# The second MLP product of the last two token groups from seven quarter products in place of eight

## The chip, the cores and the metric

The kernel runs on one core of a Trainium2 chip. The metric is the device time of one execution in microseconds (us). Three timed runs of the kernel before gave 926.75, 925.68 and 925.69 us, median 925.69 us.

## The reference

A causal attention with a window of 128 positions and a linear distance bias, followed by an MLP with SiLU, all in float32:

```
scores = scale * q @ k.T;  scores = where(0 <= rel < 128, scores + bias, -1e9)
attn = exp(scores - max);  attn = attn / (sum(attn) + 1e-9)
x = (attn @ v).transpose(0, 2, 1, 3).reshape(4608, 512)
h = x @ w_in                      # 4608 x 2048
g = h * (1 / (1 + exp(-h)))
out = g @ w_out                   # 4608 x 512
```

There are 8 batches of 8 heads, 576 positions and head size 64. Only the last line of the MLP, `g @ w_out`, is computed in another way by the change.

## The kernel before

The 4608 tokens are cut into 9 groups of 512 (`TG`), counted here from 0 to 8. A group has 16 steps (`NF`), one for each 128 of the 2048 hidden columns; the text writes step 7.3 for step 3 of group 7, and the code numbers steps through, `n = 16 * g + f`. A step has these parts:

- `gemm1`, 12 products on PE (TensorE), in two halves: 128 hidden columns of 512 tokens into a PSUM tile `h`. From group 2 on every operand is split into two fp16 parts, a high and a low one, and a product is made of three: high by high, high by low, low by high.
- `act1` on ACT (ScalarE): the tanh of `h` into the SBUF tile `gt`. `act2` on DVE (VectorE): `(gt + 1) * h`. `act3` on ACT: the fp16 part `gh`. `act4` on DVE: the fp16 rest `gl`.
- `gemm2`, 12 products: for each of four blocks of 128 tokens `gh` by the high part of `w_out`, `gh` by its low part, `gl` by the high part, each 512 columns wide, summed over the 16 steps in one PSUM bank for each block (tags w, x, y, z, one buffer each). After the last step `store` scales the four tiles and sends them out.

Each product is a weight load (LDWEIGHTS, 128 columns) and a MATMUL. In the order that is written out by hand, `gemm2` of step n-1 follows `gemm1` of step n, so that the activation of step n has the time of a `gemm2` and the next `gemm1` to finish. At the end of a group both remaining `gemm2` follow the last `gemm1`; at its start two `gemm1` stand together.

The order is a list of positions, four to a step, at each of which PE gets half of a `gemm1` or a `gemm2`. A table (`plan`, filled by `put` and `ahead`) says what else is issued at a position. The attention for group g+1 is laid between the steps of group g, one pair of heads-and-tokens (`p`) every 8 positions, that is every two steps: scores on PE, masked row maximum on DVE (L469), exponentials on ACT (L479), splits on ACT (L488) and DVE (L493), a transpose by DMA, the product with v on PE (L543), normalising on DVE (L561 to L570) and two fp16 parts (L580, L142). Queries and keys of the later batches are split on ACT (L385) and DVE (L391), v on POOL (GpSimd, L415) and DVE (L421). Group 8 has no attention beside it. All engines work through their queues in order.

The lines to follow are gemm1 L650 (L655 in the first two groups), act1 L666, act2 L671, act3 L681, act4 L687, gemm2 L719, and the stores L730 to L739.

Of the kernel before, what the change touches and what calls it, by code (L numbers as in the profile page):

```python
# [91 lines left out]
def tile_window_attention_then_silu_mlp(ctx, tc, qk, qk16, v, w_in, w_out, distance, out):  # L92
# [534 lines left out]

    hps, gact, ops = {}, {}, {}

    def gemm1(n, half):  # L630
# [4 lines left out]
        if n // NF >= IN16:
            g, w = n // NF, w16[0, f]
            for cc in (2 * half, 2 * half + 1):
                seq += [(0, 0, cc), (0, 1, cc), (1, 0, cc)]
            for i, (wp, xp, cc) in enumerate(seq):
                start, stop = half == 0 and i == 0, half == 1 and i == len(seq) - 1  # L640
                c = xp * NCC + cc
                if g > IN16:
# [6 lines left out]
                for k, (o, x) in enumerate(moves):
                    nc.tensor.matmul(o, w[:, wp, cc], x, start=start and k == 0, stop=stop, skip_group_check=True)  # L650
# [12 lines left out]
    def act1(n):  # L663
        gt = pool.tile([P, TG], F32, tag="gt", name=f"gt{n}")
        scale = 0.5 / W_SCALE if n // NF < IN16 else gsc[n // NF][:, 0:1]
        nc.scalar.activation(gt, hps[n], AF.Tanh, scale=scale)  # L666
        gact[n] = gt

    def act2(n):
        gt = gact[n]  # L670
        nc.vector.scalar_tensor_tensor(out=gt, in0=gt, scalar=1.0, in1=hps[n], op0=ALU.add, op1=ALU.mult)  # L671

    def act3(n):
        gt = gact[n]
        dt = F32R if n // NF < OUT16 else F16
        gh = pool.tile([P, TG], dt, tag="gh", name=f"gh{n}")
        gl = pool.tile([P, TG], dt, tag="gl", name=f"gl{n}")
        if n // NF < OUT16:
            (nc.vector.tensor_copy if at_edge(n) else nc.scalar.copy)(gh, gt)  # L679
        else:  # L680
            nc.scalar.activation(gh, gt, AF.Copy, scale=CUT)  # L681
        gact[n] = (gh, gl, gt)

    def act4(n):
        gh, gl, gt = gact[n]
        if n // NF >= OUT16:
            nc.vector.scalar_tensor_tensor(out=gl, in0=gt, scalar=CUT, in1=gh, op0=ALU.mult, op1=ALU.subtract)  # L687
            return
        minus(nc.vector if at_edge(n) or n < NF else nc.gpsimd, gl, gt, f32(gh))

    def turn_over(n):
# [8 lines left out]
        if more:  # L700
            x_parts(i, 1)
            for k in range(1, GT):
                x_parts(i + k, 0)
                x_parts(i + k, 1)

    def gemm2(n, half):
        g, f = divmod(n, NF)
        for ti in (2 * half, 2 * half + 1):
            if f == 0:
                ops[ti] = psum.tile([P, DM], F32, tag="wxyz"[ti], name=f"o{g}_{ti}")  # L710
            gh, gl, _ = gact[n]
            t = slice(ti * P, (ti + 1) * P)
            if g < OUT16:
                hi, lo = weight("woh", f), weight("wol", f)
            else:
                hi, lo = w16[1, f][:, 0], w16[1, f][:, 1]
            seq = [(gh, hi), (gh, lo), (gl, hi)]
            for i, (a, w) in enumerate(seq):
                nc.tensor.matmul(  # L719
                    ops[ti], a[:, t], w, start=(f == 0 and i == 0), stop=(f == NF - 1 and i == len(seq) - 1),  # L720
                    skip_group_check=True,
                )
# [344 lines left out]
```

## Time and profile before

| | |
|---|---|
| median of three runs | 925.69 us |
| the profiled execution's own time | 926.23 us |
| its span from the first to the last instruction | 924.4 us |
| PE busy | 914.6 us (99%) |
| DVE busy | 645.0 us (70%) |
| ACT busy | 559.6 us (61%) |
| POOL busy | 116.0 us (13%) |
| TensorE clock granted | 1.00 of full speed |

How it is read: a busy share is an average over stages. A product is shown with the time from its start to the end of its results (0.38 us for 512 columns), while the next one starts before that; what a product costs is therefore read from the distance of two starts. "Idle before" is the time an engine stood still ahead of an instruction, and behind the arrow stands what ended it. In the views in order of time, equal instructions that follow each other are merged into one row with their count.

### The profile page before, as it was taken

The numbers are of one execution on the slowest core, as the hardware profiler recorded it, in microseconds if no ns is written. First come the engines' busy times: TensorE is split into PE (matmuls) and PEld (weight loads), VectorE is DVE, ScalarE is ACT, GpSimd is POOL, SyncE is SP. The second block draws the span as 40 slices with busy tenths as digits, with TensorE's granted clock in tenths as the row PEclk, the third lists the DMA queues.
The fourth block names the chain that finished last, engine by engine and source line by source line (L and its number), as shares of the span: only waits on it lengthen the run. The fifth ranks groups of instructions, "written<-read, shape, count | busy, mean of one in ns | idle before, by whom it ended". The sixth has DMA issues, their size and how long they took to land.

```text
span 924.4 us, 17093 instructions
## 1 busy us (share of the span) xinstructions
PE 914.6 (99%) x6426; PEld 572.4 (62%) x6426; DVE 645.0 (70%) x1629; ACT 559.6 (61%) x1149; POOL 116.0 (13%) x115
## 2 busy tenths in 40 slices
PE   9999999999999999999999999999999999999998
PEld 8867777777787886555555555555555555544443
DVE  6889876446776778888788778666867777743222
ACT  7778997675556764666677755555655565533222
POOL 2343442222221220000000000000000000000000
PEclk9999999999999999999999999999999999999999
DMA  8977825243275645434598736444545454211001
GB/s 311 392 189 225 256 57 129 69 91 80 71 218 152 178 115 137 114 94 112 114 247 219 203 88 163 112 103 104 160 115 115 114 160 113 65 35 52 1 1 45
DMA packets 197747, 122.89 MB, mean 133 GB/s; under 512 B 166432, under 2 KB 166816, under 8 KB 197664
## 3 DMA queue, kind: packets, MB, share of 16 engines
q1 hardware_dynamic: 197376, 121.54, 49.3%
q8 instruction: 50, 0.82, 0.4%
q14 instruction: 33, 0.27, 0.1%
q10 hardware_dynamic: 288, 0.26, 0.1%
HBM read 71.96 MB, written 9.44 MB: 88 GB/s over the span
## 4 chain that ended last, share of the span: by engine, by line
PE 85%; DVE 5%; ACT 1%; issue 1%; ACTq 0%
PE o L719 38%; PE h L650 29%; PE h L655 8%; PE av L543 4%; PE sp L439 3%; PE sp L446 2%; DVE gt L671 1%; DVE hr L493 1%; DVE t L469 0%; DVE w L816 0%; DVE vmx L204 0%; ACT t L479 0%; DVE x L142 0%; ACT w L804 0%; DVE wr L810 0%
## 5 line engine op out<-in xcount | busy, mean ns | idle before, releaser
L719 PE MATMUL o<-w,gh 128*128 128x512 f16 (+1 forms) x1152 | 351.2, 386 | 0.0
L650 PE MATMUL h<-xt,w 128*128 128x512 f16 (+1 forms) x1536 | 310.5, 353 | 0.0
L650 PEld LDWEIGHTS <-w 128*128 128x128 f16 x1536 | 144.6, 98 | 125.8 <-issue 2.2
L666 ACT ACTIVATE gt<-h,gsc 128x512 f32<-128x512 f32 x112 | 77.0, 687 | 239.8 <-PE h L650 237.7
L719 PE MATMUL o<-w,gl 128*128 128x512 f16 (+1 forms) x576 | 221.6, 385 | 0.2 <-DVE gl L142 0.2
L671 DVE SCALAR_TENSOR_TENSOR gt<-gt,h 128x512 f32<-128x512 f32 x144 | 98.7, 686 | 147.3 <-ACT gt L666 146.8
L719 PEld LDWEIGHTS <-gh 128*128 128x128 f16 x768 | 74.8, 98 | 89.1
L479 ACT ACTIVATE t<-t,mx 128x256 f32<-128x256 f32 (+1 forms) x288 | 125.2, 486 | 5.2 <-DVE mx L469 5.0
L493 DVE SCALAR_TENSOR_TENSOR hr<-t,hr 128x512 f16<-128x512 f32 (+1 forms) x128 | 89.3, 703 | 29.7 <-ACT hr L488 29.6
L687 DVE SCALAR_TENSOR_TENSOR gl<-gt,gh 128x512 f16<-128x512 f32 x96 | 66.8, 696 | 42.4 <-ACT gh L681 41.3
L655 PE MATMUL h<-xh,w 128*128 128x512 f32 x256 | 89.8, 405 | 0.0
L719 PEld LDWEIGHTS o<-w,gh 128*128 128x128 f32 x384 | 69.8, 188 | 15.3 <-DVE vsc L264 0.3
L415 POOL TENSOR_SCALAR v<-rv,vsc 128x512 f16<-128x512 f32 x30 | 25.2, 841 | 427.8 <-DMA rv<-v 351.8
L681 ACT ACTIVATE gh<-gt 128x512 f16<-128x512 f32 x96 | 60.4, 629 | 28.1 <-DVE gt L671 23.7
L488 ACT ACTIVATE hr<-t 128x512 f16<-128x512 f32 (+1 forms) x128 | 71.4, 595 | 1.4 <-DVE hr L493 1.4
L719 PEld LDWEIGHTS <-gl 128*128 128x128 f16 x384 | 37.6, 98 | 46.2 <-DVE gl L687 1.2
L543 PEld LDWEIGHTS <-hl 128*128 128x128 f16 x1464 | 51.4, 98 | 16.5 <-issue 5.2
L469 DVE CUSTOM_DVE_ANT_0 t<-sp,tab,vsc 128x256 f32<-128x256 f32 (+1 forms) x144 | 58.5, 461 | 1.8 <-PE sp L439 1.4
L140 POOL TENSOR_TENSOR gl<-gt,gh 128x512 fp32r<-128x512 f32 x30 | 38.6, 1286 | 164.2 <-ACT gh L679 148.9
L543 PE MATMUL av<-v,hl 128*128 128x65 f16 (+1 forms) x1464 | 54.8, 193 | 1.6 <-DVE mx L469 1.5
L655 PEld LDWEIGHTS h<-xh,w 128*128 128x128 f32 x256 | 48.1, 188 | 12.3 <-issue 0.2
L469 DVE CUSTOM_DVE_ANT_0 t<-sp,tab 128x256 f32<-128x256 f32 (+1 forms) x144 | 50.1, 402 | 3.3 <-PE sp L446 2.9
(135 smaller groups left out, 1006.5 us busy)
## 6 DMA issues: line engine op xcount, KB each, us to landing
r<-qk SPq DMA_DIRECT2D x36, 512.0 KB, 3.9
qs<-qk SPq DMA_DIRECT2D x18, 512.0 KB, 5.1
out<-ot SPq DMA_DIRECT2D x35, 256.0 KB, 2.4
wr<-w_in SPq DMA_DIRECT2D x16, 512.0 KB, 6.7
wr<-w_out SPq DMA_DIRECT2D x16, 512.0 KB, 6.2
rv<-v SPq DMA_DIRECT2D x30, 256.0 KB, 4.0
vm<-v SPq DMA_DIRECT2D x27, 256.0 KB, 5.0
q<-qk SPq DMA_DIRECT2D x18, 256.0 KB, 3.3
```

The costliest lines, as they stand in the source:

```text
L469: nc.vector.tensor_tensor_reduce(out=st[p]["t"][u][:, h, 2 * P - n :], in0=st[p]["sp"][h][:, u, o].rearrange("p o c -> p (o c)"), in1=tab[ ...
L479: nc.scalar.activation(x, x, AF.Exp, bias=st[p]["mx"][:, 2 * u + h : 2 * u + h + 1], scale=-1.0)
L488: nc.scalar.activation(split_of(p, u, hr)[:, 0], t[:, :, 2 * P - n :], AF.Copy, scale=PSCALE)
L493: nc.vector.scalar_tensor_tensor(out=hr[:, 1], in0=t[:, :, 2 * P - n :], scalar=PSCALE, in1=hr[:, 0], op0=ALU.mult, op1=ALU.subtract)
L543: nc.tensor.matmul(av[:, 2 * u + h, : rhs.shape[-1]], lhs, rhs, start=(n == 0), stop=(n == len(seq) - 1), skip_group_check=True,)
L650: nc.tensor.matmul(o, w[:, wp, cc], x, start=start and k == 0, stop=stop, skip_group_check=True)
L655: nc.tensor.matmul(hps[n], w[:, cc], x, start=(half == 0 and i == 0), stop=(half == 1 and i == len(seq) - 1), skip_group_check=True,)
L666: nc.scalar.activation(gt, hps[n], AF.Tanh, scale=scale)
L671: nc.vector.scalar_tensor_tensor(out=gt, in0=gt, scalar=1.0, in1=hps[n], op0=ALU.add, op1=ALU.mult)
L681: nc.scalar.activation(gh, gt, AF.Copy, scale=CUT)
L687: nc.vector.scalar_tensor_tensor(out=gl, in0=gt, scalar=CUT, in1=gh, op0=ALU.mult, op1=ALU.subtract)
L719: nc.tensor.matmul(ops[ti], a[:, t], w, start=(f == 0 and i == 0), stop=(f == NF - 1 and i == len(seq) - 1), skip_group_check=True,)
```

## The change

In groups 7 and 8 (`FAST`) `gemm2` uses a scheme of seven products for a 2 by 2 split of both operands. The tokens are taken 256 at a time (two blocks of 128), the hidden columns as pairs of blocks j and j+8, the output columns in two halves of 256. A step now is one pair j for one 256 tokens: 8 steps for the first 256 tokens, then 8 for the second. `gemm1_fast` fills the same PSUM tile `h` with block j+8 in the first half and block j in the second, in 24 products of 256 columns. `act2` adds three instructions on DVE, which form five sums and differences of the four blocks; `act3` and `act4` work on seven blocks in two instructions each (256 and 640 columns). `gemm2_fast` makes 7 times 3 products of 256 columns into four PSUM banks (the seven sums, two to a bank). After 8 steps `store_fast` joins the seven sums to four quarters: two copies on ACT and eight instructions on DVE, half of them behind the first four products and the rest behind the others, and sends two tiles of 128 by 512.

The sums of w_out's quarters that the seven products need are made at eight places in groups 4 (its last position) to 6 (`SUMS`, `SUMS_STEP`): each has seven instructions on POOL, two on ACT and two on DVE, and puts its fp16 results into buffers that are free by then.

In the order, step 8 of such a group keeps `gemm2` of step 7 behind it, step 9 has no `gemm2`, and step 10 has those of steps 8 and 9; the rest is as before.

```diff
+FAST = (NG - 2, NG - 1)
+SUMS, SUMS_STEP = 316, 16
...
+    def sum_float(j):
+        wsum["r"] = r = pool.tile([P, 2, DM], F32, tag="big", name=f"wr{j}")
+        for k in range(2):
+            w = w16[1, j + k * HALF_F]
+            nc.gpsimd.tensor_add(r[:, k], w[:, 0], w[:, 1])
+
+    def sum_make(j):
...
+        nc.gpsimd.tensor_sub(q[:, 0], b12, b22)
+        nc.gpsimd.tensor_sub(q[:, 1], b21, b11)
+        nc.gpsimd.tensor_add(q[:, 2], b11, b22)
+        nc.gpsimd.tensor_add(q[:, 3], b21, b22)
+        nc.gpsimd.tensor_add(b11, b11, b12)
...
+    def sum_hi(j):
+        sum_tiles(j)
+        nc.scalar.activation(wsum[0, j][:, :, 0], wsum["q"], AF.Copy, scale=0.5)
+        nc.scalar.activation(wsum[1, j][:, 0], wsum["r"][:, 0, : DM // 2], AF.Copy, scale=-0.5)
...
+    def gemm1_fast(n, half):
+
+        g, (t, j) = n // NF, divmod(n % NF, HALF_F)
+        w = w16[0, j + HALF_F * (1 - half)]
+        out = hps[n][:, half * TG // 2 : (half + 1) * TG // 2].rearrange("p (t c) -> p t c", t=2)
+        seq = [(wp, xp, cc) for cc in range(NCC) for wp, xp in ((0, 0), (0, 1), (1, 0))]
...
+    PARTS = (slice(0, 2), slice(2, 7))
...
     def act2(n):
-        gt = gact[n]
+        gt = gact[n][:, :TG]
         nc.vector.scalar_tensor_tensor(out=gt, in0=gt, scalar=1.0, in1=hps[n], op0=ALU.add, op1=ALU.mult)
+        if n // NF in FAST:
+            a = gact[n].rearrange("p (a c) -> p a c", c=P)
+            gact[n] = a
+            pairs = a[:, 0:4].rearrange("p (a b) c -> p a b c", b=2)
+            nc.vector.tensor_sub(a[:, 6:8], pairs[:, :, 0], pairs[:, :, 1])
+            nc.vector.tensor_add(a[:, 4:6], a[:, 2:4], a[:, 0:2])
+            nc.vector.tensor_add(a[:, 3], a[:, 2], a[:, 1])
...
+            for k in PARTS:
+                nc.scalar.activation(gh[:, k], gt[:, 1:][:, k], AF.Copy, scale=0.5 * CUT)
...
+            for k in PARTS:
+                nc.vector.scalar_tensor_tensor(
+                    out=gl[:, k], in0=gt[:, 1:][:, k], scalar=0.5 * CUT, in1=gh[:, k], op0=ALU.mult, op1=ALU.subtract
+                )
...
+    def gemm2_fast(n, half):
+        g, (t, j) = n // NF, divmod(n % NF, HALF_F)
+        gh, gl, _ = gact[n]
+        for k in range(4) if half == 0 else range(4, 7):
...
+            seq = [(gh, hi), (gh, lo), (gl, hi)]
+            for i, (a, w) in enumerate(seq):
+                nc.tensor.matmul(
+                    product(k), a[:, k], w, start=j == 0 and i == 0 and k % 2 == 0,
...
+        if half == 0:
+            copy(0, m5)
+            join(ot[0][:, right], m3, once[:, 0], ALU.add)
+            join(ot[0][:, left], m1, once[:, 0], ALU.subtract)
+            join(ot[0][:, left], m4, ot[0][:, left], ALU.add)
+            return
+        copy(1, m2)
+        join(ot[1][:, left], m4, once[:, 1], ALU.add)
+        join(ot[1][:, right], m1, once[:, 1], ALU.subtract)
+        join(ot[1][:, right], m3, ot[1][:, right], ALU.add)
+        join(ot[0][:, left], m7, ot[0][:, left], ALU.add)
+        join(ot[1][:, right], m6, ot[1][:, right], ALU.add)
...
+                behind = [] if f == 0 else [n - 1]
+                if g in FAST and f in (HALF_F + 1, HALF_F + 2):
+                    behind = [] if f == HALF_F + 1 else [n - 2, n - 1]
```

The first place is PE in the last step of group 8: what one token block (before) and one of the seven sums (now) is made of. The names are the PSUM tile, the moving part of w_out or of its sums, and the stationary part of the activation. Before:

```order
L719 LDWEIGHTS gh_11016
L719 MATMUL o_3_10580<-w_1_7_5395,gh_11016 128x512
L719 LDWEIGHTS gh_11016
L719 MATMUL o_3_10580<-w_1_7_5395,gh_11016 128x512
L719 LDWEIGHTS gl_11017
L719 MATMUL o_3_10580<-w_1_7_5395,gl_11017 128x512
```

Now:

```order
L809 LDWEIGHTS gh_11988
L809 MATMUL m_1_6_11700<-wt_9019,gh_11988 128x256
L809 LDWEIGHTS gh_11988
L809 MATMUL m_1_6_11700<-wt_9019,gh_11988 128x256
L809 LDWEIGHTS gl_11989
L809 MATMUL m_1_6_11700<-wt_9019,gl_11989 128x256
```

Where four such blocks of three stood in a step, seven of half the width stand now, with as many weight loads as products.

The second place is the queue of DVE in group 7 at step 7.8, behind the last `gemm2` of the first 256 tokens. Before, act2, act4, the low part of x, and then the row maximum of the attention:

```order
L671 SCALAR_TENSOR_TENSOR gt_10069<-gt_10069,h_10048 128x512
L687 SCALAR_TENSOR_TENSOR gl_10081<-gt_10069,gh_10080 128x512
L142 SCALAR_TENSOR_TENSOR x_10084<-xs_10058,x_10084 128x256
L469 ISA t_0_10120,mx_10111<-sp_0_10093,tab,vsc_6995 128x256
L469 ISA mx_10111 128x1
```

Now, from the last of act2's new instructions on (`of` are the output tiles, `m` the PSUM banks, `once` the copies that ACT makes):

```order
L753 TENSOR_TENSOR gt_10397<-gt_10397 128x128
L832 SCALAR_TENSOR_TENSOR of_0_0_10417<-m_0_0_9704,gsc_9561,once_0_10419 128x256
L832 SCALAR_TENSOR_TENSOR of_0_0_10417<-m_0_2_9711,gsc_9561,once_0_10419 128x256
L832 SCALAR_TENSOR_TENSOR of_0_0_10417<-m_0_0_9704,gsc_9561,of_0_0_10417 128x256
L776 SCALAR_TENSOR_TENSOR gl_10425<-gt_10397,gh_10424 128x256
L776 SCALAR_TENSOR_TENSOR gl_10425<-gt_10397,gh_10424 128x640
L147 SCALAR_TENSOR_TENSOR x_10430<-xs_10380,x_10430 128x256
L832 SCALAR_TENSOR_TENSOR of_0_1_10418<-m_0_0_9704,gsc_9561,once_0_10419 128x256
L832 SCALAR_TENSOR_TENSOR of_0_1_10418<-m_0_2_9711,gsc_9561,once_0_10419 128x256
L832 SCALAR_TENSOR_TENSOR of_0_1_10418<-m_0_0_9704,gsc_9561,of_0_1_10418 128x256
L832 SCALAR_TENSOR_TENSOR of_0_0_10417<-m_0_4_9729,gsc_9561,of_0_0_10417 128x256
L832 SCALAR_TENSOR_TENSOR of_0_1_10418<-m_0_6_9736,gsc_9561,of_0_1_10418 128x256
```

The eight joins now stand in the middle of a group, ahead of the row maximum and of act2 of the next step.

The third place is the end of DVE's queue, step 8.15. Before:

```order
L671 SCALAR_TENSOR_TENSOR gt_11013<-gt_11013,h_11000 128x512
L687 SCALAR_TENSOR_TENSOR gl_11017<-gt_11013,gh_11016 128x512
L736 TENSOR_SCALAR ot_1_11041<-o_1_10568,gsc_10501 128x512
L731 TENSOR_SCALAR ot_3_11053<-o_3_10580,gsc_10501 128x256
```

Now the activation of this step, without the eight joins, the same as above, that follow it:

```order
L746 SCALAR_TENSOR_TENSOR gt_11982<-gt_11982,h_11957 128x512
L751 TENSOR_TENSOR gt_11982<-gt_11982 128x256
L752 TENSOR_TENSOR gt_11982<-gt_11982 128x256
L753 TENSOR_TENSOR gt_11982<-gt_11982 128x128
L776 SCALAR_TENSOR_TENSOR gl_11989<-gt_11982,gh_11988 128x256
L776 SCALAR_TENSOR_TENSOR gl_11989<-gt_11982,gh_11988 128x640
```

Two instructions between `h` and `gemm2` have become six, and one and a half stores behind the last product have become eight joins.

More of the change, by code (lines that the diff above doesn't have):

```diff
@@ L66 @@
 CUT = 2.0**-25
+FAST = (NG - 2, NG - 1)
+HALF_F = NF // 2
+SUMS, SUMS_STEP = 316, 16
+SUM_TAGS = tuple(f"w1_{k}" for k in range(7, 15))
+MORE_TAGS = (("w1_15", 1), ("k", KSLOTS), ("k", KSLOTS))
 STATS, CONV_IN, CONV_OUT = 66, 106, 172
@@ new lines, in gemm1_fast @@
+    def gemm1_fast(n, half):
[3 more added lines that the diff above has]
+        seq = [(wp, xp, cc) for cc in range(NCC) for wp, xp in ((0, 0), (0, 1), (1, 0))]
+        for i, (wp, xp, cc) in enumerate(seq):
+            nc.tensor.matmul(
+                out, w[:, wp, cc], xt[g, "g"][:, 2 * t : 2 * t + 2, xp * NCC + cc],
+                start=half == 0 and i == 0, stop=i == len(seq) - 1, skip_group_check=True,
+            )
@@ L704, in turn_over @@
                 x_parts(i + k, 1)
+    def gemm2_fast(n, half):
+        g, (t, j) = n // NF, divmod(n % NF, HALF_F)
+        gh, gl, _ = gact[n]
+        for k in range(4) if half == 0 else range(4, 7):
+            if j == 0 and k % 2 == 0:
+                ops[k // 2] = psum.tile([P, DM], F32, tag="wxyz"[k // 2], name=f"m{g}_{t}_{k}")
+            hi, lo = (sum_part(k, j, part) for part in range(2))
+            seq = [(gh, hi), (gh, lo), (gl, hi)]
+            for i, (a, w) in enumerate(seq):
+                nc.tensor.matmul(
+                    product(k), a[:, k], w, start=j == 0 and i == 0 and k % 2 == 0,
+                    stop=j == HALF_F - 1 and i == len(seq) - 1, skip_group_check=True,
+                )
+        if j == HALF_F - 1:
+            store_fast(g, t, half)
@@ new lines, in product, with store_fast, copy, join @@
+    def product(k):
+        return ops[k // 2][:, k % 2 * (DM // 2) : (k % 2 + 1) * (DM // 2)]
+    def store_fast(g, t, half):
+        m4, m3, m1, m5, m2, m7, m6 = range(7)
+        left, right = slice(0, DM // 2), slice(DM // 2, DM)
+        if half == 0:
+            st["ot"] = [pool.tile([P, DM], F32, tag="io", name=f"of{g}_{t}_{k}") for k in range(2)]
+            st["once"] = pool.tile([P, 2, DM // 2], F32, tag="x", bufs=4, name=f"once{g}_{t}")
+        ot, once = st["ot"], st["once"]
+        def copy(k, m):
+            nc.scalar.activation(once[:, k], product(m), AF.Copy, scale=gsc[g][:, 2:3])
+        def join(o, m, a, op):
+            nc.vector.scalar_tensor_tensor(
+                out=o, in0=product(m), scalar=gsc[g][:, 3:4], in1=a, op0=ALU.mult, op1=op
+            )
+        if half == 0:
+            copy(0, m5)
+            join(ot[0][:, right], m3, once[:, 0], ALU.add)
+            join(ot[0][:, left], m1, once[:, 0], ALU.subtract)
+            join(ot[0][:, left], m4, ot[0][:, left], ALU.add)
+            return
+        copy(1, m2)
[4 more added lines that the diff above has]
+        join(ot[1][:, right], m6, ot[1][:, right], ALU.add)
+        for k in range(2):
+            first = g * TG + (2 * t + k) * P
+            nc.sync.dma_start(out[first : first + P, :], ot[k])
@@ L896, in tile_window_attention_then_silu_mlp @@
         put(STATS + k, w_stat, k % 2, k // 2)
+    for j in range(HALF_F):
+        n = SUMS + SUMS_STEP * j
+        for k, fn in enumerate((sum_float, sum_make, sum_hi, sum_lo)):
+            put(n + 3 * k, fn, j)
     for x, wait in enumerate((0, 2, 5)):
```

56 lines of the change are left out of this document (48 added, 8 removed).

## The prediction

> **What bounds the kernel now.** I read the page first: the share of PE and the chain that ended last; then the stretches of the groups concerned.
>
> ```profile
> span 924.4 us, 17093 instructions
> PE 914.6 (99%) x6426; PEld 572.4 (62%) x6426; DVE 645.0 (70%) x1629; ACT 559.6 (61%) x1149; POOL 116.0 (13%) x115
> PE 85%; DVE 5%; ACT 1%; issue 1%; ACTq 0%
> 747.36:800.95 53.59, 53.59 (x397) 28.11 (x395) 38.98 (x96) 31.20 (x61) 2.60 (x3) 1.00 0.47 119
> 837.26:915.05 77.79, 77.79 (x362) 35.16 (x360) 21.47 (x31) 19.98 (x31) 0.00 (x0) 1.00 0.04 13
> ```
>
> The stretch rows give, after the length, the busy time of PE, weight loads, DVE, ACT and POOL, then the granted clock. PE never stands still, at full clock, so fewer products are time saved as long as PE stays the bound. In the main part of group 7 (747.36 to 800.95, steps 7.0 to 7.9) DVE has only 53.59 - 38.98 = 14.6 us to spare; in group 8 it has 56 of 78. I expect the bound to move in the first stretch.
>
> **What PE saves.** The cost of a product is the distance of starts.
>
> ```profile
> 902.10 2.75 PE L650 MATMUL h<-xt,w 128*128 128x512 f16 x12
> 907.28 2.75 PE L650 MATMUL h<-xt,w 128*128 128x512 f16 x12
> 272.88 2.79 PE L650 MATMUL h<-xt,w 128*128 128x256 f16 x24
> 275.43 0.71 PE L719 MATMUL o<-w,gh 128*128 128x512 f32 x2
> ```
>
> One step of group 8 is 24 products of 512 columns in 907.28 - 902.10 = 5.18 us: 0.216 us each. Group 2 already has gemm1 products of 256 columns, with a load each: 24 of them from 272.88 to 275.67. The last one of them lasts 0.27 to 0.28 us (a 512 product's 0.38, less half of its 0.216), so 23 distances are 2.51 us: 0.109 each. The next row's start would make it 2.55 / 24 = 0.106, but an f32 load may blur that edge. I take 0.109: two halves cost slightly more than a whole. Group for group 384 x 0.216 becomes (384 + 336) x 0.109. For both: 768 x 0.2158 = 165.7 becomes 1440 x 0.109 = 157.0: **-8.7 us** (-12.7 at 0.106). A step falls from 5.18 to 4.91 us: gemm2 2.29 for 2.59, gemm1 2.62 for 2.59.
>
> **What DVE gains in work.** The row of a two-step period in group 7, step 7.5 on:
>
> ```profile
> 774.80 0.69 DVE L671 SCALAR_TENSOR_TENSOR gt<-gt,h 128x512 f32<-128x512 f32 x1 [1.72 <-ACT gt L666]
> 775.52 0.75 DVE L391 SCALAR_TENSOR_TENSOR q<-r,vsc,q 64x512 f16<-64x512 f32 x1
> 776.30 0.69 DVE L687 SCALAR_TENSOR_TENSOR gl<-gt,gh 128x512 f16<-128x512 f32 x1
> 776.91 0.75 DVE L391 SCALAR_TENSOR_TENSOR k<-r,vsc,k 128x512 f16<-128x512 f32 x1
> ...
> 778.58 0.42 DVE L570 TENSOR_TENSOR xs<-av,r 128x256 f32<-128x256 f32 x1
> 778.92 0.68 DVE L493 SCALAR_TENSOR_TENSOR hr<-t,hr 128x512 f16<-128x512 f32 x1
> 780.70 0.69 DVE L671 SCALAR_TENSOR_TENSOR gt<-gt,h 128x512 f32<-128x512 f32 x1 [1.10 <-ACT gt L666]
> 782.08 0.69 DVE L687 SCALAR_TENSOR_TENSOR gl<-gt,gh 128x512 f16<-128x512 f32 x1 [0.69 <-ACT gh L681]
> 782.69 0.42 DVE L142 SCALAR_TENSOR_TENSOR x<-xs,x 128x256 f16<-128x256 f32 x1
> ...
> 786.77 0.69 DVE L671 SCALAR_TENSOR_TENSOR gt<-gt,h 128x512 f32<-128x512 f32 x1 [1.38 <-ACT gt L666]
> ```
>
> 512 columns take 0.69 us, 256 take 0.42; an independent instruction follows after 0.61 or 0.34, one that needs the result after the whole time and 0.03. By that slope 128 columns take 0.29 and 640 take 0.83 (estimates). The new act2 is then 0.72 + 0.34 + 0.45 + 0.25 = 1.76 us for 0.70, the new act4 0.34 + 0.74 = 1.08 for 0.61: 1.53 us more a step. The 0.69 us in which act4 waits for ACT shrinks to some 0.45: ACT's second part (640 columns) can begin only behind act2's last sum. That gap comes in every second step; in the others L391 fills it.
>
> From act2 of step 7.0 (747.36) to act4 of step 7.9 stand 10 steps: 15.3 us of such work; 5 gaps of 0.45: 2.2; and the eight joins of step 7.8, at 0.40 each and 0.1 for those that wait for one another: 3.4. DVE is done at 747.4 + 38.98 + 20.9 = 807.3, where it was done at 800.95. PE's need is read here:
>
> ```profile
> 780.21 0.38 PE L719 MATMUL o<-w,gl 128*128 128x512 f16 x1
> ...
> 803.73 0.59 PE L719 MATMUL o<-w,gh 128*128 128x512 f16 x2
> 804.16 0.38 PE L719 MATMUL o<-w,gl 128*128 128x512 f16 x1
> ```
>
> gemm2 of step 7.9 starts at 803.73; by then PE is 9 x 0.30 - 11 x 0.03 = 2.4 us early, and its ninth product (0.87 us in) is the first that reads the second part of gl: 802.2. PE waits 807.3 - 802.2 = **+5.1 us** here, whatever of it comes in earlier steps. Behind it the attention thins out, and DVE catches up. Bounds: 0, if the additions fit, and 8, if ACT's longer chain adds 0.3 us a step. The moved gemm2 of step 7.8 costs nothing: the joins that free its banks (the sixth for the first bank) end before gl of 7.9 does; without that cover it would wait some 2 us. The two stores that now leave in mid-group wait on SP for the seventh and eighth join; the transposes of hr queued behind them wait for DVE instructions that stand behind the joins anyway, and the product with v that reads them comes most of a period later, so this costs nothing. ACT's own extra (0.5 us a step) lies in its idle time, 22 of 54 us.
>
> **The ends of the groups.** The last step of group 8:
>
> ```profile
> 915.05 0.59 PE L719 MATMUL o<-w,gh 128*128 128x512 f16 x2
> 915.31 0.69 ACT L666 ACTIVATE gt<-h,gsc 128x512 f32<-128x512 f32 x1 [3.11 <-PE h L650]
> 916.03 0.69 DVE L671 SCALAR_TENSOR_TENSOR gt<-gt,h 128x512 f32<-128x512 f32 x1 [3.10 <-ACT gt L666]
> 916.75 0.63 ACT L681 ACTIVATE gh<-gt 128x512 f16<-128x512 f32 x1 [0.76 <-DVE gt L671]
> 917.41 0.69 DVE L687 SCALAR_TENSOR_TENSOR gl<-gt,gh 128x512 f16<-128x512 f32 x1 [0.69 <-ACT gh L681]
> 918.16 0.39 PE L719 MATMUL o<-w,gl 128*128 128x512 f16 x1
> ...
> 920.12 0.38 PE L719 MATMUL o<-w,gl 128*128 128x512 f16 x1
> 920.53 0.47 ACT L730 ACTIVATE ot<-o,gsc 128x256 f32<-128x256 f32 x1
> 921.04 0.48 DVE L731 TENSOR_SCALAR ot<-o,gsc 128x256 f32<-128x256 f32 x1 [1.05 <-ACT ot L730]
> 921.55 0.33 SPq L733 DMA_DIRECT2D out<-ot  x1
> ```
>
> Before, gl is read 3.11 us after the next-to-last gemm2 began, 0.09 late (14 products are 3.02). Now, from the same zero: act1 0.26 to 0.95, act2 0.98 to 2.78, gh's second part 2.83 to 3.58 (0.75, by the 0.63 above), gl's 3.61 to 4.44. PE wants it behind 29 products, at 3.16: it waits 1.3, **+1.2 us** net, and the same at the end of group 7: **+1.2**. At the start of group 8 only one gemm1 (2.62) stands between h and its gemm2: wanted at 2.62 + 0.87 = 3.49, there at 4.44: **+0.9**. In group 7 the attention's scores lie between, nothing is added. In the middle of group 8 the joins push act2 of the next step back: **+0.3** (0 to 1).
>
> The tail: the last product starts at 920.12, the span ends 4.28 us later. Now the bank of m5 is copied (0.47) when the fourth sum is through, and eight joins follow in line: the last ends 3.3 us after the last product's start, then the transfer, 921.55 to 924.4 = 2.85 before and 0.1 longer for a whole tile: 6.3 for 4.28, **+2.0 us**.
>
> **The sums in groups 5 and 6.** Each of eight places puts 1.6 us on DVE, 1.5 on ACT, 6 on POOL (two of 512 columns, five of half that). POOL is nearly idle, DVE has about 7 us in the 24 of such a place, and gl is ready 3.2 us ahead of need (776.99 in the DVE rows, first read at 780.21 by PE). A hazard shows early in the kernel:
>
> ```profile
> 160.02 1.30 POOL L140 TENSOR_TENSOR gl<-gt,gh 128x512 fp32r<-128x512 f32 x1 [2.61 <-ACT gh L679]
> 160.88 0.72 DVE L493 SCALAR_TENSOR_TENSOR hr<-t,hr 128x256 f16<-128x256 f32 x1 [1.92 <-ACT hr L488]
> 161.80 0.43 DVE L493 SCALAR_TENSOR_TENSOR hr<-t,hr 128x256 f16<-128x256 f32 x1 [0.20 <-ACT hr L488]
> ```
>
> The same DVE instruction took 0.72 us while POOL worked and 0.43 without it; it ended 0.28 after POOL's. Four DVE instructions in a burst of 6 us, held 0.3 to 1.3 us each, are 1 to 5 us a place, with 3 us of cover: I take **+0.3** for all eight, and 0 to +8 as bounds. [...]
>
> **Sum.** -8.7 + 5.1 + 1.2 + 1.2 + 0.9 + 0.3 + 2.0 + 0.3 = +2.3 us. The profiled execution took 926.2 us, 0.5 above the median of its runs; I put the change on the median: 925.7 + 2.3 = **928.0 us**.
>
> **Rivals.** First, **DVE keeps up** in group 7: the PE saving stands, only the ends cost. It decides at 802.2 - 747.4 - 38.98 = 15.8 us of added work instead of 20.9, for instance with the joins inside waits and no gaps. For it: my costs of TENSOR_TENSOR in SBUF and of 640 columns are by slope; against it: the stretch has 14.6 us to spare. Time 928.0 - 5.1 = 922.9, faster. [...] Third, **256 columns stream at 0.106**: 4 us less on PE, of which group 7's half is lost where DVE is the bound: 926.0, no difference.
>
> **Chances.** DVE-bound as summed 0.53 (924.8 to 930.5), DVE keeps up 0.25 (922 to 924.5), POOL 0.12 (931 to 935), cheap halves 0.10. A measurement can tell about 0.2%, 1.85 us. From the first case 0.34 slower and 0.19 same; from the second 0.21 faster and 0.04 same; the third slower; the fourth 0.05 faster, 0.05 same. Faster 0.26, same 0.28, slower 0.46. Cases of both signs hold much, so the range goes from 922.7 to 932.5; the likeliest case's own is 924.8 to 930.5.
>
> **What would show it.** In the profile of after: L692 and L809 products 0.109 us apart; weight loads of PE waiting for DVE's gl (L776) from step 7.3 to 7.11, about 5 us; DVE without idle time there; waits of 1.3 us at both group ends and 0.9 at the start of group 8; 6.3 us from the last product's start to the end, and groups 5 and 6 as long as before. It is wrong if PE hardly waits in group 7, or if groups 5 and 6 grow.

## The result, and the profile after

| | before | after |
|---|---|---|
| median | 926.22 us | 937.42 us (937.20 to 938.95, 4 runs) |
| ratio | | 1.0125, 95% interval 1.0113 to 1.0138 |
| span of the profiled execution | 924.4 us | 935.4 us |

Before's 926.22 is the median of four executions, one of which was an outlier of 5360.61 us; the other three are the ones named ahead of the prediction. The change makes the kernel 1.25% slower, about 11 us. The forecast was 928.0 us with a range from 922.7 to 932.5: the sign was right, the size was not. From the page after, the span, the busy shares and the chain that ended last by engine:

```profile
span 935.4 us, 18743 instructions
PE 909.7 (97%) x7098; PEld 635.4 (68%) x7098; DVE 737.5 (79%) x1805; ACT 587.9 (63%) x1200; POOL 176.9 (19%) x171
PE 70%; DVE 16%; ACT 3%; issue 2%; DMA 0%; SPq 0%; DVEq 0%; ACTq 0%
```

PE's part of the chain fell from 85% to 70%, DVE's rose from 5% to 16%. Where the 11 us arose is read from the start of each group's first `gemm1` product on PE (lengths from one such start to the next, us):

| stage | before | after | difference |
|---|---|---|---|
| group 4 | 97.22 | 99.98 | +2.8 |
| group 5 | 94.22 | 96.20 | +2.0 |
| group 6 | 95.83 | 97.07 | +1.2 |
| group 7 | 93.41 | 98.15 | +4.7 |
| group 8, to its last product | 82.86 | 80.80 | -2.1 |
| last product to the end | 4.28 | 6.58 | +2.3 |

Two of these starts, the first products of group 7 (before, then after; group 4 starts at 456.58 and 456.62):

```profile
743.85 2.75 PE L650 MATMUL h<-xt,w 128*128 128x512 f16 x12
749.87 2.78 PE L692 MATMUL h<-xt,w 128*128 128x256 f16 x24
```

Groups 4 to 6, where only the sums of `w_out` were added, lost 6.0 us. Group 7 lost 4.7 in place of the 2.0 of the forecast. Group 8 (-2.1 for -1.95) and the tail (+2.3 for +2.0) came near the forecast.

The stretch rows of after answer to those of before: group 7 from act2 of step 7.0 to the end of act4 of step 7.9, and group 8 to its last `gemm1`'s end (length; busy PE, weight loads, DVE, ACT, POOL; granted clock):

```profile
753.41:813.38 59.97, 56.68 (x624) 48.91 (x621) 56.76 (x144) 37.86 (x73) 2.68 (x3) 1.00 0.45 114
848.02:923.02 75.00, 74.36 (x681) 65.99 (x678) 49.66 (x106) 28.46 (x48) 0.00 (x0) 1.00 0.04 15
```

DVE now has 3.2 us to spare in 60. PE and DVE around its longest waits, in order of time:

```profile
809.03 0.88 PE L551 MATMUL av<-v,hl 128*128 128x65 f16 x24 [1.81 <-DVE mx L477]
812.71 0.28 PE L809 MATMUL m<-ws,gl 128*128 128x256 f16 x1 [0.29 <-DVE gl L776]
817.61 0.95 PE L447 MATMUL sp<-k,q 128*128 128x128 f16 x14 [2.46 <-DVE xs L578]
...
806.81 1.27 DVE L832 SCALAR_TENSOR_TENSOR of<-m,gsc,of 128x256 f32<-128x256 f32 x3
808.00 0.48 DVE L477 CUSTOM_DVE_ANT_0 t<-sp,tab,vsc 128x256 f32<-128x256 f32 x1
...
812.23 1.16 DVE L776 SCALAR_TENSOR_TENSOR gl<-gt,gh 128x256 f16<-128x256 f32 x2
...
817.13 0.42 DVE L578 TENSOR_TENSOR xs<-av,r 128x256 f32<-128x256 f32 x1
...
824.55 0.83 DVE L776 SCALAR_TENSOR_TENSOR gl<-gt,gh 128x640 f16<-128x640 f32 x1 [0.47 <-ACT gh L760]
```

PE waits for the attention far more than for `gl`: the product with v waits 1.81 us for the row maximum, which stands behind the joins, and the scores wait 2.46 us for their PSUM bank, which the normalising of the last pair (its result is the tile `xs`) must free first. act4 of step 7.9 ends at 812.23 + 1.16 = 813.4, as forecast (807.3, and 6.0 later by the sums), but from 791.8 to 824.1 DVE is never idle for more than 0.11 us; before that it has four gaps of 0.47 us between the two parts of act4, where five of 0.45 were forecast.

The ends, the start of group 8 and the tail on PE and DVE:

```profile
845.30 0.28 PE L809 MATMUL m<-ws,gl 128*128 128x256 f16 x1 [0.51 <-DVE gl L776]
846.59 0.28 PE L809 MATMUL m<-ws,gl 128*128 128x256 f16 x1 [0.47 <-DVE gl L776]
853.81 0.28 PE L809 MATMUL m<-ws,gl 128*128 128x256 f16 x1 [0.17 <-DVE gl L776]
855.11 0.28 PE L809 MATMUL m<-ws,gl 128*128 128x256 f16 x1 [0.47 <-DVE gl L776]
905.66 2.78 PE L692 MATMUL h<-xt,w 128*128 128x256 f16 x24
910.57 2.78 PE L692 MATMUL h<-xt,w 128*128 128x256 f16 x24
928.82 0.27 PE L809 MATMUL m<-wt,gl 128*128 128x256 f16 x1
930.87 1.26 DVE L832 SCALAR_TENSOR_TENSOR of<-m,gsc,of 128x256 f32<-128x256 f32 x3
```

A step of group 8 takes 910.57 - 905.66 = 4.91 us, the forecast's number.

### The profile page after: what moved, and what is told of

It is laid out like the page before. It is cut to its first block, busy times and chain, and to the rows that moved or that the text cites. A ratio compares the mean times of both kernels' runs of the same rounds, so it can differ in the third digit from the quotient of the medians.

```text
span 935.4 us, 18743 instructions
## 1 busy us (share of the span) xinstructions
PE 909.7 (97%) x7098; PEld 635.4 (68%) x7098; DVE 737.5 (79%) x1805; ACT 587.9 (63%) x1200; POOL 176.9 (19%) x171
## 4 chain that ended last, share of the span: by engine, by line
PE 70%; DVE 16%; ACT 3%; issue 2%; DMA 0%; SPq 0%; DVEq 0%; ACTq 0%
PE o L868 26%; PE h L720 18%; PE h L725 8%; PE h L692 6%; PE m L809 4%; PE av L551 4%; PE sp L447 2%; PE sp L454 2%; DVE hr L501 2%; DVE gt L746 2%; DVE t L477 2%; DVE gl L776 1%; DVE k L399 1%; DVE of L832 1%; DVE gl L781 1%
## 5 line engine op out<-in xcount | busy, mean ns | idle before, releaser
L868 PE MATMUL o<-w,gh 128*128 128x512 f16 (+1 forms) x896 | 275.4, 389 | 1.1 <-ACT gh L769 0.7
L720 PE MATMUL h<-xt,w 128*128 128x512 f16 (+1 forms) x1152 | 222.6, 344 | 0.0
L868 PE MATMUL o<-w,gl 128*128 128x512 f16 (+1 forms) x448 | 173.2, 387 | 0.3 <-DVE gl L147 0.2
L720 PEld LDWEIGHTS <-w 128*128 128x128 f16 x1152 | 107.6, 98 | 83.6 <-issue 2.2
L746 DVE SCALAR_TENSOR_TENSOR gt<-gt,h 128x512 f32<-128x512 f32 x144 | 98.4, 683 | 71.7 <-ACT gt L742 71.2
L501 DVE SCALAR_TENSOR_TENSOR hr<-t,hr 128x512 f16<-128x512 f32 (+1 forms) x128 | 97.4, 767 | 30.2 <-ACT hr L496 30.0
L868 PEld LDWEIGHTS <-gh 128*128 128x128 f16 x512 | 49.7, 98 | 59.8 <-ACT gh L769 1.2
L725 PE MATMUL h<-xh,w 128*128 128x512 f32 x256 | 89.9, 405 | 0.0
L692 PE MATMUL h<-xt,w 128*128 128x256 f16 x768 | 88.6, 273 | 0.0
L692 PEld LDWEIGHTS <-w 128*128 128x128 f16 x768 | 74.4, 98 | 8.7
L781 DVE SCALAR_TENSOR_TENSOR gl<-gt,gh 128x512 f16<-128x512 f32 x64 | 50.6, 790 | 25.4 <-ACT gh L769 24.5
L760 ACT ACTIVATE gh<-gt 128x256 f16<-128x256 f32 x64 | 36.9, 577 | 47.7 <-DVE gt L746 24.6
L769 ACT ACTIVATE gh<-gt 128x512 f16<-128x512 f32 x64 | 40.2, 629 | 39.3 <-DVE gt L746 38.0
```

Of the source, the lines that this page charges most:

```text
L501: nc.vector.scalar_tensor_tensor(out=hr[:, 1], in0=t[:, :, 2 * P - n :], scalar=PSCALE, in1=hr[:, 0], op0=ALU.mult, op1=ALU.subtract)
L692: nc.tensor.matmul(out, w[:, wp, cc], xt[g, "g"][:, 2 * t : 2 * t + 2, xp * NCC + cc], start=half == 0 and i == 0, stop=i == len(seq) - 1, ...
L725: nc.tensor.matmul(hps[n], w[:, cc], x, start=(half == 0 and i == 0), stop=(half == 1 and i == len(seq) - 1), skip_group_check=True,)
L868: nc.tensor.matmul(ops[ti], a[:, t], w, start=(f == 0 and i == 0), stop=(f == NF - 1 and i == len(seq) - 1), skip_group_check=True,)
```

## The experiments

Eighteen kernels ran. The theory that they tried, called A in the expectations: POOL's sums hold DVE's instructions that read two operands from SBUF, and cost time only at places where PE waits for DVE anyway; and in group 7 DVE's sum of work is the bound. Rivals are named with the runs. "Before" ran beside each and took 926.0 to 926.2 us.

| run | median us | ratio to before (95%) |
|---|---|---|
| sums_only | 931.74 | 1.0061 (1.0046 to 1.0076) |
| sums_no_pool | 926.51 | 1.0004 (0.9995 to 1.0013) |
| sums_pool_alone | 928.83 | 1.0029 (1.0018 to 1.0040) |
| pool_one_input | 927.28 | 1.0012 (1.0003 to 1.0021) |
| no_sums | 931.96 | 1.0059 (1.0042 to 1.0075) |
| group8_alone | 932.18 | 1.0066 (1.0051 to 1.0081) |
| no_additions7 | 928.77 | 1.0033 (1.0020 to 1.0046) |
| two_additions7 | 932.62 | 1.0071 (1.0057 to 1.0085) |
| joins_later7 | 938.33 | 1.0132 (1.0117 to 1.0148) |
| sums_moved | 927.19 | 1.0013 (1.0003 to 1.0022) |
| both_moved | 932.86 | 1.0071 (1.0056 to 1.0086) |
| g8_moved | 926.25 | 1.0002 (0.9993 to 1.0011) |
| g8_tail | 926.31 | 1.0001 (0.9992 to 1.0009) |
| both_moved2 | 938.65 | 1.0131 (1.0115 to 1.0146) |
| g8_moved2 | 931.59 | 1.0060 (1.0047 to 1.0074) |
| both_spaced | 936.23 | 1.0110 (1.0095 to 1.0126) |
| g8_spaced | 929.45 | 1.0037 (1.0024 to 1.0049) |
| g8_free | 926.81 | 1.0007 (0.9998 to 1.0016) |

### The sums by themselves

sums_only and no_sums cut the change in two:

```diff
-FAST = (NG - 2, NG - 1)
+FAST = ()
```

> The sums of w_out's quarters are made as in the change, but no group uses them; groups 7 and 8 run as before. The trace of the changed kernel shows the first product of group 7 6.0 us later than before, so if the sums alone do that: before + 6.0, about 932, with some 2.8 us of it ahead of group 5, 2.0 in group 5 and 1.2 in group 6. If the prediction's +0.3 for the sums was right and the 6 us come from something else in the changed kernel: before + 0.3, about 926.

no_sums drops the loop that puts the sums in the order, and `sum_part` returns a quarter of `w_out`.

> The changed kernel without the sums: the seven products read plain quarters of w_out, everything else as in the change. What the sums cost and what groups 7 and 8 cost should add up: changed kernel - 6.0, about 931.4, with group 7 still 4.7 us longer than before, group 8 2.1 shorter, and the tail 2.3 longer. If the sums cost only the 0.3 of the prediction: about 937.

The sums alone cost 5.7 us, the rest alone 5.9; together 11.6 for the 11.2 measured. (Two of the four executions of no_sums, with a granted clock of 0.997 over the run for 0.998 and 0.999, lost some 1.7 us to it, as the last section tells; the other two are 4.9 above before, which gives 10.6.) The prediction's +0.3 falls. By the group starts, sums_only lost 2.5, 2.0 and 1.3 us in groups 4, 5 and 6. Two runs then split the sums themselves. In sums_no_pool `sum_float` and `sum_make` only name other data of the same shape; in sums_pool_alone the loop is cut:

```diff
-        for k, fn in enumerate((sum_float, sum_make, sum_hi, sum_lo)):
+        for k, fn in enumerate((sum_float, sum_make)):
```

> Sums only, without their seven instructions on POOL: the two on ACT and the two on DVE at each place stay, and read other data of the same shape and type. Theory A, POOL's reads hold DVE's instructions with two SBUF inputs: nearly all of the 6 us go, before + 0 to 1. Theory B, the 1.6 us of DVE and 1.5 us of ACT at each place are what is too much: + 4 to 6 stay.

> Sums only, with the seven instructions on POOL at each place and without the two on ACT and the two on DVE that make the fp16 parts. Theory A: + 4 to 6 over before, and DVE's instructions with two SBUF inputs are long beside POOL's. Theory B: + 0 to 1.

POOL is what costs, but not by itself everywhere: POOL alone loses 2.8, ACT's and DVE's part alone 0.4, both 5.7. POOL alone loses all of it at the first place (2.66 us in group 4, 0.00 in groups 5 and 6). DVE and POOL there, from sums_pool_alone:

```profile
536.11 1.62 DVE L399 SCALAR_TENSOR_TENSOR q<-r,vsc,q 64x512 f16<-64x512 f32 x1
...
537.85 1.03 DVE L781 SCALAR_TENSOR_TENSOR gl<-gt,gh 128x512 f16<-128x512 f32 x1
538.80 1.21 DVE L399 SCALAR_TENSOR_TENSOR k<-r,vsc,k 128x512 f16<-128x512 f32 x1
539.93 1.21 DVE L501 SCALAR_TENSOR_TENSOR hr<-t,hr 128x512 f16<-128x512 f32 x1
541.06 0.54 DVE L286 TENSOR_REDUCE row<-vt 1x3 f32<-1x384 f32 x1
...
541.83 0.60 DVE L288 TENSOR_SCALAR row<-row 1x3 f32<-1x3 f32 x1
...
538.28 1.17 POOL L658 TENSOR_TENSOR wq<-wr 128x256 f32<-128x256 f32 x1
539.42 1.17 POOL L659 TENSOR_TENSOR wq<-wr 128x256 f32<-128x256 f32 x1
...
541.68 0.72 POOL L661 TENSOR_TENSOR wr<-wr 128x256 f32<-128x256 f32 x1
...
547.14 0.94 PE L447 MATMUL sp<-k,q 128*128 128x128 f16 x14 [1.77 <-DVE vsc L300]
```

The same instructions in before (q, gl, k and hr, then L283, which is L288 here):

```profile
536.17 0.75 DVE L391 SCALAR_TENSOR_TENSOR q<-r,vsc,q 64x512 f16<-64x512 f32 x1
...
537.03 0.68 DVE L687 SCALAR_TENSOR_TENSOR gl<-gt,gh 128x512 f16<-128x512 f32 x1
537.63 0.74 DVE L391 SCALAR_TENSOR_TENSOR k<-r,vsc,k 128x512 f16<-128x512 f32 x1
538.29 0.68 DVE L493 SCALAR_TENSOR_TENSOR hr<-t,hr 128x512 f16<-128x512 f32 x1
...
539.66 0.16 DVE L283 TENSOR_SCALAR row<-row 1x3 f32<-1x3 f32 x1
```

Beside the burst q, gl, k and hr end 1.13 to 1.15 us apart, the last three about midway between the ends of two of POOL's instructions, and POOL's own take 1.17 for 0.72: both pay. L286 begins the scale chain of batch 3, a row of small instructions that makes the batch's scales (`vsc`); the scores of the next batch wait for its end. In before the same scores already wait, the only wait of PE in groups 4 to 7:

```profile
544.53 0.94 PE L439 MATMUL sp<-k,q 128*128 128x128 f16 x14 [0.49 <-DVE vsc L295]
```

There is no cover at that place, so every held instruction is lost time: the last of the four ends 2.2 us later than in before, L288 adds 0.44, and together that is about the 2.66 lost. Nor does the burst stand where its position is: 316 is four positions, about 5 us, ahead of group 5, which starts at 556.41 in this run, but POOL has nothing else to do and starts at 534.92, right behind v's instruction.

By this trace q, gl, k and hr, with two operands in SBUF, are held (1.62, 1.03, 1.21 and 1.21 us for 0.75, 0.68, 0.74 and 0.68 in before); act2 (L746), with one operand from PSUM, keeps 0.69 us beside the burst. L288, with a single operand, is held all the same (0.60 for 0.16).

A last run of this kind gave POOL's seven instructions one operand each (`tensor_scalar_mul(q[:, 0], b12, 2.0)` for `tensor_sub(q[:, 0], b12, b22)` and so on).

> As sums_pool_alone, but POOL's seven instructions at each place read one operand each (a product with a constant) in place of two; shapes and places as there. If only POOL instructions with two SBUF operands hold DVE: before + 0. If any POOL instruction that reads SBUF does, DVE's q, gl, k and hr beside the burst at the first place are long again, and the cost goes with the burst's length: + 1 to 2.6.

It cost 1.2 us, and by the PE starts all of it (1.4) at the first place. Neither expectation was met whole: one-operand instructions hold DVE less (gl 0.92, hr 0.88, q and k not at all), while the small ones of the scale chain took up to 0.42 for 0.16.

### Places that cost and places that do not

In sums_only the PE starts jump at some places only: 2.5 us for the one at position 316, 0.8 for 332, 1.2 for 380, 0.8 for 396, 0.5 for 428, and nothing for 348, 364 and 412. At 380, the end of group 5, `hr`, `gl` and `v` take 1.64, 1.22 and 1.21 us beside the burst for 0.69, 0.69 and 0.75 in before; act2 of the last step comes late behind them, and the last `gemm2` of the group, which has only one other `gemm2` for cover, waits for `gh`:

```profile
649.12 0.60 PE L868 MATMUL o<-w,gh 128*128 128x512 f16 x2 [0.71 <-ACT gh L769]
```

The first attempt to use the places that cost nothing replaced the loop by a list of positions:

```diff
-    for j in range(HALF_F):
-        n = SUMS + SUMS_STEP * j
+    for j, n in enumerate(SUMS_AT):
```

> Sums only again (groups 7 and 8 as before), with the eight places at positions 340, 348, 356, 364, 372, 404, 412 and 420 in place of 316 and every sixteenth after it: none beside the scale chain of batch 3 and none at the end or in the first steps of a group. Theory A, a place costs only where the attention or gl has no time to spare there (in the sums alone the places at 316, 332, 380, 396 and 428 cost 2.5, 0.8, 1.2, 0.8 and 0.5 us, those at 348, 364 and 412 nothing): before + 0.4 to 1.5, about 927. Rival, each burst on POOL costs its share wherever it stands: before + 5 to 6.

> The whole change (groups 7 and 8, result right) with the eight places of the sums at positions 340, 348, 356, 364, 404, 412, 420 and 428, those that cost nothing in the runs before (428 cost 0.5). If the two halves of the loss add up: changed kernel - 5.2, about 932.2, with group 7 as long as in the change. Rival, what the sums no longer delay only waits longer in group 7: less than 3 us faster.

> The seven products in group 8 alone, the sums at 340, 348, 356, 364, 404, 412, 420 and 468: group 7 without its loss and the sums at places that cost nothing. By the measured parts: group 8 - 2.1, tail + 2.3, sums 0 to 0.5: before + 0.2 to 0.7, no difference that can be measured. Rival, sums cost about 0.7 a place wherever they stand: + 5.

> As g8_moved, and behind the last step the four half tiles leave each as soon as its joins are done, on two queues, in place of two whole tiles on one. The last transfer is then half as large (2.85 us for 3.27 in the traces): g8_moved - 0.4, before - 0.2 to + 0.3. If the joins are not what the last transfer waits for: no change against g8_moved.

All came near theory A: +1.1 for sums_moved, before + 0.2 for g8_moved, and both_moved 4.6 below the change, although all four of its executions had the lower clock of the last section (0.996 to 0.997 over the run). (g8_tail shows that half tiles bring nothing: its last join ends 0.4 later behind the last product, since three joins that need one another now follow each other.) But in these four kernels, whose places stand 8 positions apart, the low part of one of the five sums was made from the first sums of the next place. That frees a buffer early, so the next two runs gave each place its own:

> As both_moved, whose low part of one of the five sums was made from the next place's first sums (the places stand so close that the name was taken over); here each place keeps its own. The instructions and their order are the same: 931.2 to 932.9, that is changed kernel - 4.6 to - 6.2; if the mixed-up tile had taken a wait away, slower than that by the wait.

> As g8_moved, with each place keeping its own first sums (there the low part of one of the five was made from the next place's). Same instructions and order: 926.0 to 926.6, no difference against before; rival as for both_moved2.

The loss is back, 5.4 us in g8_moved2, and both_moved2 is 1.2 us slower than the change: with whole sums the places did cost. POOL, DVE and PE in g8_moved2:

```profile
613.85 2.50 POOL L651 TENSOR_TENSOR wr<-w 128x512 f32<-128x512 f16 x2 [5.92 <-DVE ws L681]
...
620.57 0.68 POOL L423 TENSOR_SCALAR v<-rv,vsc 128x512 f16<-128x512 f32 x1
621.29 0.75 DVE L429 SCALAR_TENSOR_TENSOR v<-rv,vsc,v 128x512 f16<-128x512 f32 x1 [1.29 <-POOL v L423]
622.73 0.53 PE L551 MATMUL av<-v,hl 128*128 128x65 f16 x12 [0.85 <-DVE mx L477]
```

A burst that waits for its buffer (5.92 us) holds v, queued behind it on POOL; DVE's part of v waits, the row maximum behind it, and PE. Two of the four waits that PE has there beyond before's come this way, 0.85 and 1.77 us; in the two others, 0.29 and 0.97, the scores wait for xs, which stands on DVE behind the sums' own two instructions and a held hr. The first kind was put down to the spacing, so three runs kept 16 positions, where a burst stands right behind v:

> The seven products in group 8 alone, with the sums 16 positions apart as in the change (each burst on POOL then stands right behind v's instruction, and v is never behind one that waits) at 284, 300, 348, 364, 412, 428, 476 and 492: the third and the fourth quarter of groups 4 to 7. If a place costs only where DVE has no time to spare or v is queued behind it: before + 0.7 (0.25 for group 8 and its tail, 0.46 for 428) and up to 1 for each of the two in group 4, where DVE is busy 24 of 30 us: 926.8 to 928.5. If any whole sum costs about 0.7 wherever it stands: 931.6, as in group8_alone.

> The whole change with two of the eight places moved, from 316 (beside the scale chain of batch 3) and 380 (the end of group 5) to 284 and 300 in group 4; the others stay, at 332, 348, 364, 396, 412 and 428. If those two cost their 2.5 and 1.2 where they were, and nothing to 1 each where they are now: changed kernel - 1.7 to - 3.7, 933.7 to 935.7. If the cost goes with the number of places: 937.4.

> The seven products in group 8 alone, whole sums, 16 positions apart, at 332, 348, 364, 396, 412, 428, 476 and 492: no burst and no DVE instruction of a sum between the reduction of batch 3's scales and the scores that use them, and none at a group's last position. If the sums' cost belongs to those places: before + 0.2 to 0.9 (group 8 -2.1, tail +2.3, sums 0 to 0.5), 926.2 to 926.9. If what was free in g8_spaced was so only because the two places in group 4 had been paid for: 929 to 931.6.

In g8_spaced the places at 348, 364, 412, 428, 476 and 492 cost 0.1 us together, by the PE starts; the one at 300 delayed the row maximum by 1.2, and the scale chain was 1.9 late, though no burst stood there. DVE there, in g8_spaced:

```profile
539.40 1.22 DVE L681 SCALAR_TENSOR_TENSOR ws<-wq,ws 128x1024 f16<-128x1024 f32 x1
540.54 0.83 DVE L681 SCALAR_TENSOR_TENSOR wt<-wr,wt 128x256 f16<-128x256 f32 x1
541.29 0.68 DVE L501 SCALAR_TENSOR_TENSOR hr<-t,hr 128x512 f16<-128x512 f32 x1
541.89 0.54 DVE L286 TENSOR_REDUCE row<-vt 1x3 f32<-1x384 f32 x1
```

Now it was the sums' own two DVE instructions, ahead of the chain. both_spaced gave back 1.2 us: by its PE starts the sums still cost 3.5, of which 3.1 at the same two points and 0.4 at 428, and all its executions had the lower clock that the last section tells of (0.996 to 0.997 over the run). g8_free has no place near the chain nor at a group's end, and eight whole sums cost 0.35 us in its trace: +0.7 us in all, no difference that can be measured. So the sums' 6 us belong to places, shown with whole sums.

Why 332 and 396 cost 0.8 us each behind 316 and 380, and nothing without them, no run tried apart, but the traces differ. In sums_only the two DVE instructions of place 316 (ws and wt, 567.13 to 568.68) stand ahead of hr and xs, the burst for 332 waits 1.82 us until ws has read its buffer, and then holds hr (1.64 us); xs comes too late for the scores:

```profile
571.10 0.95 PE L447 MATMUL sp<-k,q 128*128 128x128 f16 x14 [0.32 <-DVE xs L578]
```

In g8_free no place stands before 332, and xs ends at 565.3, 3.2 us before the scores start. At 396 sums_only shows the same two waits, 1.82 and 0.25 us.

### Group 7

> The change with FAST = group 8 alone, the sums as in the change. If the parts add up (sums 5.7, group 8 between its first and last product -2.1, tail +2.3): before + 5.9, about 932.0, and group 7 as long as before. If group 7 was long because of something that the sums left behind and not because of the seven products: about 937.

group8_alone came out at + 6.1; its group 7 takes 93.4 us, as before: group 7 is long by its own seven products. no_additions7 takes the additions away:

```diff
+            if n // NF == NG - 2:
+                return
             pairs = a[:, 0:4].rearrange("p (a b) c -> p a b c", b=2)
```

and act3 and act4 read `a[:, 3:4].to_broadcast([P, 5, P])` there; two_additions7 leaves out the first `tensor_sub` alone.

> The change without the three additions of act2 in group 7; parts 4 to 7 of the activation repeat part 3, so that ACT and DVE still read and write as many columns in act3 and act4. This takes 1.06 us a step off DVE, 12.7 us over steps 7.0 to 7.11. Theory A, DVE's total work in group 7 holds PE there: the 7.9 us go, and the 1.2 at the end of group 7 shrink with the shorter chain, changed kernel - 7.5 to - 9, about 929. Rival, the joins that stand ahead of the row maximum at step 7.8 are what holds PE: only - 1 to - 3.

> The change without one of act2's three additions in group 7 (the difference of 256 columns); parts 6 and 7 of the activation are replaced by parts that are there, so act3 and act4 keep their columns. A dose of the run without all three, which took 8.7 us off: 0.34 us less a step on DVE, 4.1 us over steps 7.0 to 7.11. If every microsecond of DVE's sum is one of PE's waiting: changed kernel - 3.5 to - 4.5, about 933.4. If the loss has a threshold (PE waits only because one instruction is just too late): - 1 or less, or already - 7.

Against the change they took 8.7 and 4.8 us off; by the PE starts group 7 takes 89.9 and 94.2 us for 98.2. One addition less is 4.1 us less of DVE (0.34 us in each of twelve steps) and 4.0 us less of group 7. All three are 12.7 us of DVE, more than there was to lose: group 7 is 8.3 us shorter and within 0.8 of 93.4 - 4.35, PE's own time. Up to that floor, in the two doses tried, it goes microsecond for microsecond, with no threshold. What PE still waits for in group 7, first in two_additions7, then in no_additions7 (in total, times, longest):

```profile
PE sp L447 <- DVE xs L578: 1.7, 1, 1.7
PE av L551 <- DVE mx L477: 1.5, 1, 1.5
PE m L815 <- DVE gl L782: 1.0, 3, 0.5
...
PE m L816 <- DVE gl L783: 0.8, 3, 0.5
PE sp L447 <- DVE xs L578: 0.2, 1, 0.2
```

joins_later7 changes the order alone:

```diff
-            store_fast(g, t, half)
+            if g == NG - 2 and t == 0:
+                put(pos[0] + 3 - half, store_fast, g, t, half)
+            else:
+                store_fast(g, t, half)
```

> The change with the eight joins of the first 256 tokens of group 7 issued behind the row maximum of the next pair in place of ahead of it; nothing is left out. Theory A, DVE is without idle time from step 7.1 to 7.11 and its sum of work decides, not the order in it: the 1.8 us for which the product with v waits for the row maximum go, and PE waits as much longer at the next scores: changed kernel + - 0.4. Rival, the order decides: - 1.5 to - 2.

The wait for the row maximum went, and two others came, 1.58 us for the joins and 1.07 for `gl`; the scores that wait last start at 817.78 for 817.61. Its four executions took 937.4, 937.6, 939.1 and 939.2 us: the first two are the change's time (clock 0.998 and 0.999), the others lost some 1.6 us to the clock (0.997, last section). The order inside DVE's queue moves the waits and not their end.

## Why the prediction was wrong

Step by step, with the forecast first:

- **PE's saving, -8.7 us: right.** 256 columns at 0.109 us, a step of 4.91 us; group 8 with its waits is 2.1 us shorter, forecast 1.95 (-4.35 + 0.9 + 0.3 + 1.2).
- **The sums, +0.3: wrong, 6.0 measured.** This step failed. It counted a cover of 3 us for `gl` at each place and took all eight places alike. The hazard that it named, the hold by POOL, is what happens, but the cover of `gl` was not the one that counts: at the first place the held instructions stand ahead of the scale chain, and before's trace had PE waiting 0.49 us for that very chain. A second error is in the place: "The sums in groups 5 and 6" took a burst to start at its position, while POOL, idle ahead of it, ran it as soon as v was done. Among the chances POOL had 0.12, with 931 to 935 us; measured, five places cost 0.5 to 2.5 us and three nothing.
- **DVE as the bound of group 7, +5.1: right mechanism, wrong size.** Measured: 4.74 + 4.35 - 1.2 = 7.9, at the bound of 8. DVE's durations for 128 and 640 columns, 0.29 and 0.83 us, were right. Its time at act4 of step 7.9 was right to 0.1 us, but with some luck: 56.8 us busy and 3.2 idle, where the forecast had 57.7 and 2.2. Wrong was "Behind it the attention thins out, and DVE catches up": steps 7.10 and 7.11 carry a whole pair, DVE falls behind further until 824, and PE's last and longest wait is there, not at `gl` of step 7.9. What PE waits for was wrong too: the scores and the product with v share two PSUM banks with what DVE still has to read, and those come before `gl`.
- **The ends, +1.2 each, and the start of group 8, +0.9: right.** PE loses 0.67 + 0.63 = 1.30 at each end against the distance of 0.109 between products, 1.2 more than the 0.09 before; at the start it loses 0.33 + 0.63 = 0.96. The middle of group 8, +0.3: no wait at all.
- **The tail, +2.0: 2.3.** The last join ends 932.13 - 928.82 = 3.3 us after the last product's start, as forecast; the transfer takes 3.27 for 2.95.
- **Nothing for the moved gemm2 of step 7.8: right in the change.** With the joins behind the row maximum its cover was gone, and it waited 1.58 us, near the 2 given for that.

The sum with what was measured: -8.7 + 7.9 + 1.2 + 1.2 + 1.0 + 0 + 2.3 + 6.0 = +10.9, for 11.0 between the spans.

No version that ran beats the kernel before. With the sums free, group 8 alone gives back in its start, its end and its tail (1.0 + 1.2 + 2.3) what its 4.35 us of products save.

## What to carry to other kernels

Work laid "beside" a bound engine is priced at each place, by the chain that has the least cover there: look in the trace of before for the waits that the bound engine already has, however short, and keep new instructions away from what ends them, on their own engine and on another one whose reads hold it, as POOL's held DVE's here (hr 1.21 us for 0.68). When an engine in order has no idle time left, its sum of work is the cost, and the last place where it is still behind decides, so carry the sum on until it has idle time again (in two_additions7 4.1 us less of DVE were 4.0 us less of group 7); the order inside its queue only chose which wait showed it (joins_later7: the last scores at 817.78 us for 817.61). A queued burst need not wait for its place in the program: in sums_pool_alone POOL, with nothing else to do, started it at 534.92 us, right behind v's instruction and some 16 us ahead of that place.

## What the runs showed of the hardware

- In sums_pool_alone, from 538.8 to 541.1 us, DVE and POOL read SBUF side by side and their instructions ended in turn: hr on DVE, with two SBUF operands, took 1.21 us for 0.68 in before, wq on POOL 1.17 for the 0.72 of L661, a pair every 1.13 us.
- Behind the longest wait in group 7 the granted clock fell in some executions and not in others. In no_sums the wait was 2.02 us, the 24 products after it took 4.45 us for 2.78, and stretches of 3.41 us show the clock (no_sums, then after):

```profile
812.38 4.45 PE L690 MATMUL h<-xt,w 128*128 128x256 f16 x24
809.52:812.93 3.41, 1.39 (x21) 1.29 (x21) 3.31 (x9) 1.19 (x3) 0.00 (x0) 1.00 0.28 64
812.93:816.34 3.41, 3.41 (x19) 2.35 (x17) 2.88 (x11) 0.00 (x0) 0.00 (x0) 0.50 0.54 119
...
813.55:816.97 3.42, 1.60 (x15) 1.28 (x14) 3.32 (x8) 2.19 (x4) 0.40 (x1) 1.00 0.00 0
816.97:820.38 3.41, 2.77 (x33) 2.57 (x34) 3.38 (x8) 0.41 (x2) 0.00 (x0) 1.00 0.34 77
```

After's profiled execution had a wait of 2.46 us at the same place, and the same 24 products took 2.79. A stretch of 3.41 us at a clock of 0.50 is 1.7 us lost (an estimate from the second row); the 24 products took 4.45 - 2.78 = 1.67 us longer, and the two groups of times lie 1.9 us apart in no_sums (930.8 and 931.1; 932.8 twice) and 1.6 in joins_later7, whose profiled execution took 4.45 us for these products behind a wait of 2.17. The lower clock shows in the profiled executions of three more kernels: 0.59 from 818 to 822 us in joins_later7, 0.60 from 812 to 816 in both_moved, 0.71 from 816 to 820 in both_spaced. The length of the wait alone does not tell them apart: the clock fell behind 2.02 and 2.17 us and stayed behind after's 2.46. What decides it was not shown.
